# Other matrix products during attention as halves of 64 rows beside a score or a maximum

## The chip, the cores and the metric

The kernel runs on one core of a Trainium2 chip. TensorE multiplies matrices, VectorE and ScalarE read its results from PSUM, GpSimd works on SBUF alone, and SyncE (SP) issues transfers. The metric is the device time of one execution in microseconds (us), before: 1993.56, the median of three runs from 1993.28 to 1995.21.

## The reference, cut to what matters

The input has 2048 rows of 512. A condition vector gives six modulation rows; then comes one attention block of 32 heads of 16 and one mixer block with token shifts and an MLP.

```python
def _A_ref(x, wqkv, wo):
    qkv = (x @ wqkv).reshape(B, S, 3, H, Dh)...
    scores = jnp.einsum("bhqd,bhkd->bhqk", q, k) * (Dh ** -0.5)
    o = jnp.einsum("bhqk,bhkd->bhqd", _softmax(scores), v)
    return o... @ wo
def _B_ref(x, w1, w2, w3, w4):
    h = _gelu(_layernorm(x) @ w1)
    ...                                  # four column groups, shifted by +1, -1, +2, -2 rows
    x1 = x + hs @ w2
    return x1 + _gelu(_layernorm(x1) @ w3) @ w4
mod = (_silu(c) @ w_mod).reshape(c.shape[0], 6, 1, -1)
h = _layernorm(x) * (1 + ca) + sa
x = x + ga * _A_ref(h, A_wqkv, A_wo)
h = _layernorm(x) * (1 + cb) + sb
x = x + gb * _B_ref(h, B_w1, B_w2, B_w3, B_w4)
```

## The kernel before, in words

Every operand is kept as a high and a low part, and a full product is three matmuls per 128 rows of the sum (high by high, high by low, low by high; lines 361, 363 and 365), so a sum over 512 rows is 12 matmuls into one PSUM bank.

Attention runs over 64 units: four chunks of 512 queries, and 16 pairs of heads in each. The two heads of a pair lie on the two halves of the 128 rows: rows 0 to 63 hold one head's queries and keys, with their low parts and the shift, and rows 64 to 127 the other's. A unit has 16 steps over 128 keys. At each step TensorE makes, for both heads, the scores (tile `sc`, L1042), ScalarE writes their exponential into a probability tile (`pt`, L1038), GpSimd forms the low part of both heads at once (L1093; line 146 on ScalarE when GpSimd is behind), and TensorE adds up the weighted sum (`pv`, L1119 with the high part, L1116 with the low), four matmuls at a time on 32 columns each. The softmax's shift needs the maxima first: 24 steps ahead, TensorE makes other scores for maxima (`mb`, L1026), which VectorE reduces (`mx`, L1022). A score of one head and a maximum of the other head stand beside each other, as two products of 64 rows on the two halves of the array (`row_pair`).

All other matrix work of the program is fitted in between, as generators: the projections for later units (`q`, `k`, `v`), and for a chunk that is through attention the output projection (`wo`), the token mixer (`w1`, `w2`), the MLP (`w3`, `w4`) and transposes. They use all 128 rows of the array. Seven PSUM banks are shared by scores, maxima and these products; an eighth holds `pv`.

A planner in Python (`Sched`), run when the program is built, writes every instruction out in a fixed order per engine. It keeps a clock for each engine from a table of costs and has three modes for TensorE: `r` (row pairs), `c` (weighted sums) and `o` (others), with a planned cost for a change of mode (`SWITCH`, `ENTER`). `budget` pays credit per step from the due times `DUES`; in the loop, up to `GRP` row pairs are written as a burst, then weighted sums that are ready, or others as far as slack and credit go (`one` takes the next matmul of a generator).

```python
def row_pair(s, j):
    if 0 <= s < NS:
        parts.append((j, score_part(s, j)))
    if s + LEAD < NS:
        parts.append((1 - j, max_part(s + LEAD, 1 - j)))
```

The weights of these products come through a ring of three buffers (`wr`) on SP's queue, which also loads the keys, queries and V (`kst`, `qtl`, `vst`) in its order.

## Time and profile before

| | before |
|---|---|
| median of three runs | 1993.56 us |
| the profiled execution | 1993.19 us |
| its span (first to last instruction) | 1991.4 us |
| granted TensorE clock, mean | 0.991 |
| busy: TensorE, VectorE, ScalarE, GpSimd | 97%, 84%, 74%, 84% |
| TensorE matmuls in the profile | 14,480 |
| DMA, mean over the span | 147 GB/s |

A row of the groups reads: line, engine, operation, written tile `<-` read tiles, the shapes, the count; then busy time in us and the mean of one in ns; then the engine's idle time just before these instructions and what ended most of it. `64*128` before a matmul's shape are the rows and columns of the array that it uses. PEld is TensorE's weight load, shown as an engine of its own. The shown end of a matmul is modelled, so times between matmuls are read from start to start. A waits row reads: engine and line, what it waited for, us in total, how often, the longest.

### The profile page before, as it was taken

To read this page: it belongs to the slowest core of one execution; us is meant where nothing else is said; L and a number is where in the kernel's file an instruction comes from. 1 tells how busy PE (TensorE), PEld (TensorE's weight loads), DVE (VectorE), ACT (ScalarE), POOL (GpSimd) and SP (SyncE) were. 2 spreads that over 40 slices of the span, in tenths; PEclk is the share of its full clock that TensorE was granted. 3 is DMA by queue.
4 is the path that set the end of the run, shared out by engine and by line. 5 is a ranking of instruction groups with operands and counts; after the bars stand their busy time and mean duration, and the time that the engine had idled before them with its cause. 6 is when DMAs were issued, how large, how long until landed. Compare 5 with 4: busy or idle time off the path is not lost.

```text
span 1991.4 us, 42269 instructions
## 1 busy us (share of the span) xinstructions
PE 1933.8 (97%) x14480; PEld 1137.1 (57%) x14480; DVE 1669.9 (84%) x3010; ACT 1483.2 (74%) x3081; POOL 1671.0 (84%) x1601
## 2 busy tenths in 40 slices
PE   6989999999999999999999999999999999999899
PEld 4654565555445555555455555555555555555798
DVE  6969878899999888998999988888998888892643
ACT  5366888788878777787888877787888777786443
POOL 5368999999999998998898999888898988897532
PEclk8999999999999999999999999999999999999999
DMA  5675788786533433434433333344433334433432
GB/s 180 193 209 177 217 254 249 252 271 206 163 103 115 136 109 112 145 127 132 133 114 111 108 112 101 110 140 132 157 115 103 96 112 136 132 100 108 186 143 91
DMA packets 233082, 293.23 MB, mean 147 GB/s; under 512 B 125876, under 2 KB 178052, under 8 KB 216580
## 3 DMA queue, kind: packets, MB, share of 16 engines
q1 hardware_dynamic: 232868, 290.53, 45.8%
q8 instruction: 115, 1.88, 0.4%
q14 instruction: 99, 0.81, 0.1%
HBM read 225.81 MB, written 62.91 MB: 145 GB/s over the span
## 4 chain that ended last, share of the span: by engine, by line
PE 69%; DVE 9%; POOL 6%; ACT 6%; DMA 2%; issue 2%; SPq 1%; POOLq 0%; ACTq 0%; DVEq 0%
PE mb L1026 14%; PE sc L1042 11%; PE pv L1119 10%; PE w L361 7%; PE w L363 7%; PE w L365 7%; PE pv L1116 6%; DVE mx L1022 6%; POOL pt L1093 4%; ACT pt L1038 3%; PE ot L1151 1%; SPq L125 1%; DMA wr<-Ws 1%; PE q L365 1%; PE q L361 1%
## 5 line engine op out<-in xcount | busy, mean ns | idle before, releaser
L1022 DVE TENSOR_REDUCE mx<-mb 128x1 f32<-128x512 f32 x2048 | 1283.7, 682 | 117.2 <-PE mb L1026 88.6
L1093 POOL TENSOR_SCALAR pt<-pt 128x1024 f16<-128x1024 uint16 x980 | 1301.2, 1369 | 82.1 <-ACT pt L1038 78.6
L1038 ACT ACTIVATE pt<-sc 128x512 int32<-128x512 f32 x2048 | 1102.1, 602 | 272.5 <-PE mb L1026 181.2
L1026 PE MATMUL mb<-kst,qtl 64*128 64x512 f32 x2048 | 754.0, 455 | 18.3 <-DVE mx L1022 7.0
L1042 PE MATMUL sc<-qtl,kst 64*128 64x512 f32 x2048 | 728.3, 445 | 1.6 <-ACT pt L1038 0.7
L1026 PEld LDWEIGHTS mb<-kst,qtl 64*128 64x128 f32 x2048 | 347.1, 192 | 228.6 <-DVE mx L1022 108.4
L1042 PEld LDWEIGHTS sc<-qtl,kst 64*128 64x128 f32 x2048 | 334.9, 185 | 155.9 <-issue 52.5
L1119 PE MATMUL pv<-pt,vst 128*32 128x512 f16 x4096 | 348.8, 392 | 5.5 <-DMA vst<-Vs 4.9
L1116 PE MATMUL pv<-pt,vst 128*17 128x512 f16 (+1 forms) x2048 | 215.7, 397 | 4.6 <-POOL pt L1093 4.3
L1453 POOL TENSOR_TENSOR g<-xs,g 128x256 fp32r<-128x256 f32 (+2 forms) x144 | 103.4, 719 | 92.7 <-ACT g L1452 88.7
L1119 PEld LDWEIGHTS <-vst 128*32 128x32 bf16 x4096 | 112.3, 94 | 112.3 <-issue 48.1
L361 PE MATMUL w<-A,wr 128*128 128x256 f32 (+2 forms) x576 | 172.0, 299 | 0.6 <-ACT A L355 0.3
L363 PE MATMUL w<-A,wr 128*128 128x256 f32 (+2 forms) x576 | 170.0, 295 | 0.5 <-DVE A L351 0.3
L365 PE MATMUL w<-A,wr 128*128 128x256 f32 (+2 forms) x576 | 169.2, 294 | 0.0
L1116 PEld LDWEIGHTS <-vst 128*17 128x17 f16 (+1 forms) x2048 | 56.0, 90 | 130.5 <-issue 113.2
L361 PE MATMUL w<-wr,g 128*128 128x512 f32 x288 | 119.9, 416 | 0.8 <-ACT g L1452 0.6
L361 PEld LDWEIGHTS w<-A,wr 128*128 128x128 f32 x576 | 109.5, 190 | 18.0 <-issue 11.3
L365 PE MATMUL w<-wr,g 128*128 128x512 f32 x288 | 118.1, 410 | 0.2 <-POOL g L1453 0.2
L363 PEld LDWEIGHTS w<-A,wr 128*128 128x128 f32 x576 | 109.5, 190 | 14.4 <-issue 13.0
L363 PE MATMUL w<-wr,g 128*128 128x512 f32 x288 | 117.5, 408 | 0.0
L365 PEld LDWEIGHTS w<-A,wr 128*128 128x128 f32 x576 | 109.4, 190 | 12.9 <-issue 12.9
L1449 ACT ACTIVATE sq<-w 128x256 f32<-128x256 f32 (+2 forms) x144 | 55.8, 388 | 66.8 <-PE w L365 65.3
(150 smaller groups left out, 2095.6 us busy)
## 6 DMA issues: line engine op xcount, KB each, us to landing
wr<-Ws SPq DMA_DIRECT2D x80, 1024.0 KB
kst<-Ks SPq DMA_DIRECT2D x189, 256.0 KB
vst<-Vs SPq DMA_DIRECT2D x252, 192.0 KB
qtl<-Qs SPq DMA_DIRECT2D x192, 64.0 KB
Vs<-vt SPq DMA_DIRECT2D x32, 384.0 KB
Ws<-wq SPq DMA_DIRECT2D x40, 256.0 KB
Ws<-wst SPq DMA_DIRECT2D x40, 256.0 KB
wst<-in_B_w_dram SPq DMA_DIRECT2D x36, 256.0 KB
```

The lines of the kernel that those rows point to most:

```text
L361: te.matmul(o, lh, rh, start=first, stop=False)
L363: te.matmul(o, lh, rl, start=False, stop=False)
L365: te.matmul(o, ll, rh, start=False, stop=last)
L1022: end = sch.crit("D", 605, e + PX, lambda: dve.reduce_max(mxs[u][:, j, g, c:c + 1], b, axis=AX.X))
L1026: return ready, lambda: te.matmul(b, lhs, kst[u % 3][r, c * CH:(c + 1) * CH], start=True, stop=True), after
L1038: ea = sch.crit("A", 480, e + PX, lambda: act.activation(pt[s][:, j], b, AF.Exp))
L1042: return ready, lambda: te.matmul(b, kst[u % 3][r, kt * P:(kt + 1) * P], qst[u][r], start=True, stop=True), after
L1093: e_low[s] = XP["G"] + sch.crit("G", 1345, ready, lambda: pool.tensor_scalar(o, i, 0.5, 1.0, op0=OP.mult, op1=OP.mult))
L1116: te.matmul(acc[r:r + n, :], v[:, (kt + i) % 4, c - n:c].bitcast(F16), pt[s + i].bitcast(F16)[:, j, 0::2], start=False, stop=kt == NKT - 2 ...
L1119: te.matmul(acc[r:r + 32, :], v[:, kt % 4, r:r + 32], pt[s].bitcast(F16)[:, j, 1::2], start=kt == 0, stop=False, skip_group_check=True)
L1449: sch.chain(("A", cA(n), lambda: act.activation(sq, b, AF.Square, scale=2.0)), ("D", cD(n), cube), ("A", cA(n), lambda: act.activation(sq, ...
L1453: ("G", cG(n), lambda: pool.tensor_tensor(lo, xs, hi, op=OP.subtract)), (None, 0, end), bank=b)
```

## The change

During attention a sum of another product is no longer written as full matmuls. It becomes a `Group`: each of its matmuls is split in two of 64 rows, one on each half of the array, both adding into the same bank. The loop writes a half (`Group.half`, line 126) together with one score or maximum on the other 64 rows (`slot`). A product of 512 columns is one half per slot, of 256 columns two, of 128 columns four. All halves of one side can come first; when a sum goes over to the other side, a `drain` of TensorE is put ahead. What can't be paired is written whole (`Group.rest`, line 148), as is everything outside attention (line 448). The two row halves now have counters of their own (`yl`), up to `STAG` steps apart, so a score no longer needs a maximum beside it. One such sum is open at a time (`OPENS`). Planner constants go with it, among them `LACT`, how far GpSimd must be behind ScalarE before ScalarE forms a low part. Weights of the ring are released when the sums that read them are through (`settled`).

The built order has, in attention, 4832 halves, 443 drains and 666 matmuls that stay full. TensorE's order in the two places named below; names end in buffer numbers, and drains are not listed.

A product of `w3` with 256 columns, before: two row pairs, then the full product's matmuls.

```order
L1026 MATMUL mb_11624<-kst2_801,qtl2_799 128x512
L1042 MATMUL sc_11623<-qtl0_151,kst0_153 128x512
L1042 MATMUL sc_11631<-qtl0_151,kst0_153 128x512
L1026 MATMUL mb_11632<-kst2_801,qtl2_799 128x512
L363 MATMUL w3_11585<-A_10064,wr_10653 128x256
L365 MATMUL w3_11585<-A_10064,wr_10653 128x256
```

And now, behind the last matmul of a weighted sum: two halves, a score on the other rows, two halves, a maximum on the other rows.

```order
L1224 MATMUL pv_20303<-pt5_618,vst1_610 32x512
L126 MATMUL w3_20344<-A_18372,wr_20124 128x256 x2
L1139 MATMUL sc_20367<-qtl2_765,kst2_767 128x512
L126 MATMUL w3_20344<-A_18372,wr_20124 128x256 x2
L1122 MATMUL mb_20373<-kst0_153,qtl0_151 128x512
```

The matmuls of the product moved from a stretch of their own into the row stretch, two for one, and each score or maximum stands alone beside them.

A product of `w3` with 128 columns (it occurs in the first chunk alone), before:

```order
L1042 MATMUL sc_10175<-qtl0_151,kst0_153 128x512
L1026 MATMUL mb_10177<-kst2_801,qtl2_799 128x512
L361 MATMUL w3_10185<-A_9801,wr_9938 128x128
L363 MATMUL w3_10185<-A_9801,wr_9938 128x128
L365 MATMUL w3_10185<-A_9801,wr_9938 128x128
```

And now:

```order
L1122 MATMUL mb_11034<-kst2_767,qtl2_765 128x512
L126 MATMUL w3_10998<-A_10801,wr_10390 128x128 x4
L1139 MATMUL sc_11048<-qtl0_151,kst0_153 128x512
L126 MATMUL w3_10998<-A_10801,wr_10390 128x128 x4
L1139 MATMUL sc_11068<-qtl0_151,kst0_153 128x512
```

Here four halves stand beside one score.

The diff, cut to its core; the generators of the products now hand their list of matmuls to `summed`, and what followed a sum is passed along as a function.

```diff
-BTOP, BLOW = 1200.0, 300.0
+BTOP, BLOW = 1200.0, 100.0
...
-LACT = 800.0
+LACT = 4000.0
...
-EARLY, STAY, BACK, GRACE = 300.0, 300.0, 150.0, 0.0
-OWE, CTOP, OMIN, OMINC, OFIRST = 1500.0, 7000.0, 0.0, 800.0, 1500.0
-CHIGH, CMIN, CMOST, PTLOW, PLAG = 6500.0, 4, 6, 2, 1
...
+EARLY, BACK = 0.0, 400.0
...
+OWE, CTOP, CMIN, PTLOW = 0.0, 7000.0, 4, 1
+CTAKE, CIDLE = 0.0, 2
...
+STAG, OPENS = 4, 1
+DRAIN, FRESH = 150.0, 30.0
...
+class Group:
+    def __init__(self, sch, b, ops, m, t, fin):
+        self.sch, self.b, self.t, self.fin = sch, b, t, fin
+        self.parts = [ops[i:i + m] for i in range(0, len(ops), m)]
+        self.did, self.lane, self.done = [0, 0], None, False
+    def can(self, h):
+        return self.did[h] < len(self.parts)
+    def swaps(self, h):
+        return self.lane is not None and self.lane != h
+    def left(self, h):
+        return self.did[h] < len(self.parts)
+    def half(self, h):
+        r = slice(64 * h, 64 * h + 64)
+        ops = self.parts[self.did[h]]
+        first = not sum(self.did)
+        self.did[h] += 1
+        swap = self.swaps(h)
+        self.lane = h
+        last = sum(self.did) == 2 * len(self.parts)
+        for i, (lhs, rhs) in enumerate(ops):
+            if swap and not i:
+                self.sch.te.drain()
+            self.sch.te.matmul(self.b, lhs[r], rhs[r], start=first and not i, stop=last and i == len(ops) - 1, skip_group_check=True)
+        self.sch.credit -= self.t / 2
+        self.sch.spent += self.t / 2
...
+    def rest(self):
+        sch, n = self.sch, len(self.parts)
+        lag = self.did.index(min(self.did))
+        if self.did[0] != self.did[1]:
+            sch.to("r")
+            while self.did[0] != self.did[1]:
+                self.half(lag)
+                sch.T["P"] += self.t
+        while self.did[0] < n:
+            i = self.did[0]
+            for k, (lhs, rhs) in enumerate(self.parts[i]):
+                sch.te.matmul(self.b, lhs, rhs, start=not i and not k, stop=i == n - 1 and k == len(self.parts[i]) - 1, skip_group_check=True)
+            self.did = [i + 1, i + 1]
+            sch.spend(self.t)
...
+    def summed(nm, n, get, fin, ahead=None):
+        yield sch.room
+        b = dbank(nm)[:, :n]
+        ops, m = get(), CH // n
+        if not sch.carrying:
+            for i, (lhs, rhs) in enumerate(ops):
+                te.matmul(b, lhs, rhs, start=not i, stop=i == len(ops) - 1)
+                yield nsq(n)
+            fin(b)
+            return
+        g = Group(sch, b, ops, m, m * nsq(n), fin)
+        yield g
...
+    def slot(hs, g):
 
         parts = []
-        if 0 <= s < NS:
-            parts.append((j, score_part(s, j)))
-        if s + LEAD < NS:
-            parts.append((1 - j, max_part(s + LEAD, 1 - j)))
-        parts = [x for _, x in sorted(parts, key=lambda x: x[0])]
-
-        def mms():
-            for _, mm, _ in parts:
+        for h in sorted(hs):
+            k, i = divmod(yl[h], 2)
+            yl[h] += 1
+            parts.append((max_part if i else score_part)(k + LEAD * i, h))
+        if g:
+            def mms(mm=parts[0][1]):
+                g.half(1 - hs[0])
                 mm()
-        e = sch.put("P", CROW, max(x[0] for x in parts), mms)
-        return [partial(x[2], e) for x in parts]
+            if g.swaps(1 - hs[0]):
+                sch.T["P"] += FRESH if sch.fresh else DRAIN
+            e = sch.put("P", max(CROW, g.t), parts[0][0], mms)
+            g.close()
+        else:
+            e = sch.put("P", CROW, max(x[0] for x in parts), lambda: [x[1]() for x in parts])
+        sch.fresh = False
+        for x in parts:
+            x[2](e)
+        if second:
+            second.pop(0)()

...
+    def part(h):
+        while yl[h] < end:
+            k, i = divmod(yl[h], 2)
+            if i and k + LEAD >= NS or not i and k < 0:
+                yl[h] += 1
+                continue
+            break
+        if yl[h] >= end or k > seen + STAG:
+            return False
+        if i:
+            return (k + LEAD) // NKT in qst
+        if ("shift", k // NKT) not in done:
+            return None
+        return k in pt or bool(pts)
...
+        if sch.credit > CTAKE:
+            while not all(any(g.left(h) for g in sch.groups) for h in range(2)) and sch.one():
+                if sch.T["P"] > now:
+                    break
+            if sch.T["P"] > now:
+                fillers()
+                continue
+        ok = [part(h) for h in range(2)]
+        low = int(yl[1] < yl[0])
+        if sch.mode != "r":
+            lane = low
+        hs, g = [], None
+        if sch.credit > CTAKE:
+            for h in (lane, 1 - lane):
+                g = ok[h] and next((g for g in sch.groups if g.can(1 - h)), None)
+                if g:
+                    hs = [h]
+                    break
+        if not g:
+            hs = [h for h in (low, 1 - low) if ok[h]]
...
+        cap = nc_ == len(pvs) or nc_ >= CMOST or nc_ and not pvs[nc_][1] and pvs[nc_][0] % NKT == 0
+        want = sch.mode == "r" and not g and sch.groups and sch.credit > CTAKE
+        if nc_ and (cap or nc_ >= CMIN and len(pts) <= PTLOW or not hs or nc_ >= CIDLE and (want or slack > 0 and room >= nc_ * CCOL + 2 * SWITCH + ENTER - BACK)):
+            do_cols(nc_)
+        elif hs and slack <= 100.0:
+            sch.to("r")
+            sch.T["P"] = max(sch.T["P"], one)
+            if g:
+                lane = hs[0]
+            late = sorted(e_exp)
+            slot(hs, g)
+            for q in late:
+                p_low(q)
+        elif hs:
+            sch.T["P"] = now + 50.0
...
```

More of the change, by code (lines that the diff above doesn't have):

```diff
@@ L107, in __init__ @@
         self.end = 0.0
-        self.mode = None
+        self.mode, self.te, self.carrying = None, None, False
+        self.groups, self.fresh, self.opens = [], False, set()
         self.banks(8)
@@ L201, in add, with spend, one @@
         self.gens.insert(len(self.gens) if at is None else at, [gen, None])
-    def one(self):
+    def spend(self, v):
+        self.credit -= v
+        self.spent += v
+        if self.mode:
+            self.to("o")
+        self.T["P"] += v
+    def one(self, force=False):
         self.marks()
+        if self.groups and (force or not self.carrying) and self.groups[0].rest():
+            return True
         for g in list(self.gens):
@@ L301, in step @@
             self.misc(e, max(t, self.T[e]) + 500)
-        while self.T["P"] < t and self.one():
+        while self.T["P"] < t and self.one(True):
             pass
@@ L1008, in bank @@
         return x, ap_.tile([P, CH], F32, name=nm, tag=f"s{x}", bufs=1)
+    left = {}
     def max_part(m, j):
@@ L1378, in norm_T, with wo_out @@
             yield from transposed(lambda k, j: xn[key, ts[j]][:, k * P:(k + 1) * P], range(KT), len(ts), A)
[L1380 to L1392 removed]
+        def wo_out(b, i, t):
             x1 = x1t[t]
@@ L1647, in do_cols @@
     def do_cols(n):
+        while second:
+            second.pop(0)()
         sch.to("c")
@@ L1680 @@
-        now, row, slack = sch.T["P"], False, LATE
-        if can:
-            need = (s >= 0) + (s + LEAD < NS)
-            sch.flush(need)
-            free = sorted(sm.t)
-            one = free[need - 1 + 2 * (s < 0)]
+            before(seen)
+            sch.credit = max(min(sch.credit + budget(seen), CTOP), -OWE)
+        sch.flush(2)
+        now = sch.T["P"]
+        if sch.credit > CTAKE:
[5 more added lines that the diff above has]
+                continue
@@ L1686 @@
+        slack = room = LATE
+        if hs:
+            one = free[len(hs) - 1]
             if one >= LATE:
-                one = free[need - 1]
-            enter = (sch.mode != "r") * (SWITCH + ENTER)
+                one = free[0]
+                hs = hs[:1]
+            slack = one - enter - now
+            room = max(one, sch.T["D"] - CROW - PX - EARLY) - now
         else:
@@ L1694 @@
         nc_ = cols()
-        if can:
-            if sch.mode == "r" and burst < GRP:
-                slack = one - now
-                row = slack <= STAY
-            else:
-                st = one
-                for k in range(2, GRP + 1):
-                    if need * k <= len(free) and free[need * k - 1] < LATE:
-                        st = max(st, free[need * k - 1] - (k - 1) * CROW)
-                dry = sch.T["D"] if s + LEAD < NS else sch.T["A"]
-                slack = max(st, dry - CROW - PX - EARLY) - enter - now
-                row = slack <= BACK and (sch.mode == "r" or sch.credit < CHIGH and not (nc_ >= CMIN and len(pts) <= PTLOW))
```

252 lines of the change are left out of this document (120 added, 132 removed).

## The prediction, made before the result was known

> **What bounds the kernel now.** I read the page first: the share of each engine, the chain that ended last, and the costliest groups.
>
> ```profile
> span 1991.4 us, 42269 instructions
> PE 1933.8 (97%) x14480; PEld 1137.1 (57%) x14480; DVE 1669.9 (84%) x3010; ACT 1483.2 (74%) x3081; POOL 1671.0 (84%) x1601
> PE 69%; DVE 9%; POOL 6%; ACT 6%; DMA 2%; issue 2%; SPq 1%; POOLq 0%; ACTq 0%; DVEq 0%
> L1022 DVE TENSOR_REDUCE mx<-mb 128x1 f32<-128x512 f32 x2048 | 1283.7, 682 | 117.2 <-PE mb L1026 88.6
> L1093 POOL TENSOR_SCALAR pt<-pt 128x1024 f16<-128x1024 uint16 x980 | 1301.2, 1369 | 82.1 <-ACT pt L1038 78.6
> ```
>
> TensorE holds 69% of the chain, and 97% "busy" is no measure of what is left, because the ends of matmuls are modelled and overlap. VectorE and GpSimd are at 84% each over the span. So two things can set attention's length: how densely TensorE's order is packed, and how steadily the two other engines are fed. The list by tile dates attention: the first row of maxima at 63.3 us, the last matmul of the weighted sum at 1828.4 us.
>
> ```profile
> L1026 PE MATMUL mb<-kst,qtl x2048: 383/498/792, 63.3 to 1791.2; 64*128 64x512 f32 x187
> L1116 PE MATMUL pv<-pt,vst x2048: 385/397/423, 107.4 to 1828.4; 128*17 128x512 f16 x95, 128*25 128x512 f16 x92
> ```
>
> That is 1765 us. A timeline of TensorE shows what a step costs; the first column is the start, and the differences of starts are what counts.
>
> ```profile
> 1299.66 0.40 PE L1119 MATMUL pv<-pt,vst 128*32 128x512 f16 x4
> 1299.99 0.49 PE L1042 MATMUL sc<-qtl,kst 64*128 64x512 f32 x1
> ...
> 1300.34 0.62 PE L1042 MATMUL sc<-qtl,kst 64*128 64x512 f32 x2
> 1300.56 0.39 PE L1026 MATMUL mb<-kst,qtl 64*128 64x512 f32 x1
> 1300.88 0.50 PE L363 MATMUL w<-wr,g 128*128 128x512 f32 x1
> 1301.22 0.40 PE L365 MATMUL w<-wr,g 128*128 128x512 f32 x1
> 1301.45 0.60 PE L1151 MATMUL ot<-ident,ac 128*128 128x128 f32 x4
> ...
> 1303.20 0.28 PE L365 MATMUL w<-A,wr 128*128 128x256 f32 x1
> 1303.33 0.28 PE L361 MATMUL w<-A,wr 128*128 128x256 f32 x1
> 1303.53 0.50 PE L1026 MATMUL mb<-kst,qtl 64*128 64x512 f32 x1
> ```
>
> A pair of row products, or one full product of 512 columns, follows the last in 0.22 to 0.23 us (1300.34 to 1300.56, 1301.22 to 1301.45): I call 0.23 a slot. From rows to full products it takes 0.32 (1300.56 to 1300.88), so the switch costs 0.09, and the second product then starts 0.34 behind the first, another 0.11: 0.20 together. From the weighted sum to rows it is 0.33 and then 0.35: 0.10 + 0.12, so 0.21 on the mean. A switch to the weighted sum I price at 0.10, like the first part of the others.
>
> The program's order, counted from the first maximum to the last weighted sum, has 827 stretches of rows, 447 of full products, 516 of weighted sums; 2062 row slots; 1922 full slots (984,064 columns); 1536 groups of four weighted-sum products. So: 3984 x 0.23 = 916; 1536 x 0.23 = 353; switches 827 x 0.21 + 447 x 0.20 + 516 x 0.10 = 315; and 14 for narrow products (below). That is 1598 us; the other 167 us of the 1765 are waits.
>
> ```profile
> ACT pt L1038 <- PE mb L1026: 181.2, 250, 3.0
> ...
> PEld mb L1026 <- DVE mx L1022: 108.4, 299, 1.9
> ...
> DVE mx L1022 <- PE mb L1026: 88.6, 169, 2.3
> POOL pt L1093 <- ACT pt L1038: 78.6, 124, 3.7
> ACT pt L1038 <- PE sc L1042: 70.1, 102, 2.9
> ...
> PE pv L1119 <- DMA vst<-Vs: 4.9, 3, 2.7
> ```
>
> The waits go both ways: TensorE waits for VectorE to free a bank (108.4), while ScalarE, VectorE and GpSimd wait for products and for each other. That is the picture of a bursty order: three row pairs arrive in 0.7 us, and then a run of full products or weighted sums brings nothing.
>
> **The change, part by part.** *Switches.* In the changed order there are 557 stretches of rows, 103 of full products, 498 of weighted sums. Saved: 270 x 0.21 + 344 x 0.20 + 18 x 0.10 = 57 + 69 + 2 = 128 us.
>
> *Slots.* 4832 half products stand in the row stretches (3260 half slots of 512 columns), 137,216 columns (268 slots) stay full. If both halves of the array were always filled, nothing would change. They are not: walked through in order, with each half of the rows taking its own products, the row stretches need 3848 slots where 3678 would do. With the 268, that is 4116 against 3984: +132 x 0.23 = +30 us. No row of before shows a half product beside a score. The nearest is the score beside the maximum at 1300.34, two 64-row products in one slot; I take that. Instructions: 2416 more matmuls, each with its own weight load. The loads of the two row halves start together:
>
> ```profile
> 1005.08 0.19 PEld L1026 LDWEIGHTS mb<-kst,qtl 64*128 64x128 f32 x1 [0.24 <-DVE mx L1022]
> 1005.08 0.18 PEld L1042 LDWEIGHTS sc<-qtl,kst 64*128 64x128 f32 x1
> 1005.19 0.19 PEld L1026 LDWEIGHTS mb<-kst,qtl 64*128 64x128 f32 x1
> ```
>
> and the next on the same half 0.11 later. A slot whose half product comes as two of 256 columns needs two loads on that side, 0.22 in 0.23: it just fits, so 0 extra.
>
> *Narrow products.* A product of 256 columns follows in 0.12 to 0.13 (1303.20 to 1303.33), 0.005 over half a slot. One of 128 columns takes 0.11, twice its share:
>
> ```profile
> 703.08 0.28 PE L365 MATMUL w<-A,wr 128*128 128x128 f32 x1
> 703.19 0.28 PE L361 MATMUL w<-A,wr 128*128 128x128 f32 x1
> ```
>
> Before, 168 of these cost 168 x 0.053 = 9 us over their slots. Now 336 halves go four to a slot, which lasts 0.44 instead of 0.23: 84 x 0.21 = 18, so +9. The 1320 slots of two 256-wide halves last 0.24 instead of 0.23 (+12, where the full ones cost some 6): +6. Together +15 us.
>
> *Drains.* 443 stand in attention, and none before, so the price has to be bounded. 230 follow a weighted sum, where the switch empties the array anyway; 213 stand among row products. Low: nothing behind a switch, and 0.09 among rows, the first part of a switch: 19 us. High: a matmul shown for 0.40 whose successor starts after 0.23 has 0.17 to run; then a first matmul is shown 0.11 longer (0.50 against 0.39), and the second follows 0.11 late: 0.39 among rows, 0.17 behind a switch: 83 + 39 = 122 us. I take a whole switch (0.20) among rows, since that also empties and refills the array, and 0.05 behind one: 43 + 12 = 54 us. Queued behind a drain stands all of TensorE's order: the score beside it, then its exponential on ScalarE, the low part on GpSimd, and the weighted sum. The Trainium skill (TensorEngine Tiling, Key Properties) says that changing the tiling mode drains TensorE. By that the 230 behind a switch would cost nothing and the sum would be 12 us less; the 0.09 of the row-to-full switch agrees with a drain there, but no row shows an explicit one.
>
> TensorE's own work thus changes by -128 + 30 + 15 + 54 = -29 us, to 1569. From the drains' bounds: -64 to +39.
>
> *Waits.* 344 of 447 runs in which no score comes are gone, so the 88.6 and 181.2 above should shrink. How far the others can follow is read from the windows (busy PE, PEld, DVE, ACT, POOL):
>
> ```profile
> 400.00:800.00 400.00, 392.25 (x3043) 212.77 (x3041) 363.33 (x647) 323.19 (x666) 372.23 (x349) 1.00 0.47 151
> 800.00:1200.00 400.00, 396.14 (x3121) 218.71 (x3121) 362.50 (x660) 324.62 (x674) 361.43 (x348) 1.00 0.39 122
> 1200.00:1600.00 400.00, 395.07 (x3103) 221.07 (x3101) 360.88 (x654) 318.00 (x658) 360.72 (x347) 1.00 0.38 119
> 450.00:500.00 50.00, 49.78 (x376) 25.25 (x368) 46.41 (x76) 40.13 (x80) 48.14 (x41) 1.00 0.63 205
> 500.00:550.00 50.00, 49.24 (x405) 23.71 (x402) 48.40 (x84) 43.77 (x88) 47.73 (x41) 1.00 0.58 181
> ```
>
> From 400 to 1600 us GpSimd is busy 1094 of 1200 (91%), VectorE 1087. The best stretch, 450 to 550, has GpSimd at 95.9 of 100. At that pace the 1200 would last 1094 / 0.959 = 1141: at most -59 there. The remaining 565 us of attention are less loaded on these engines; I give them only TensorE's share, 29 x 565 / 1765 = 9. So the limit set by the others is -68, and the waits can fall by 39 at most. Against it: the two exponentials of a probability tile stand further apart in the new order (2.1 scores on the mean, 1.5 before), so each of the 8 tiles is held longer. I take 25 of the 39.
>
> *The rest.* Behind attention stand 12,288 more columns, 24 slots: +5.5 us, uncovered, since that stage is full products alone. The raised threshold for handing the low part to ScalarE moves the count from 980 to 976 on GpSimd: 4 x 1.4 = 5 us there, inside its 9% slack. The loads of the next weights are issued when a sum is settled; SP's queue waits in order, with the V, Q and K loads behind:
>
> ```profile
> SPq L125 <- PE w L365: 194.2, 42, 19.0
> ```
>
> TensorE now waits 4.9 us for V in all, since those loads are asked for a unit ahead; that lead is the cover, and I take 0. Were it gone, the wait would at most repeat what SP's queue now loses on one such product, 194.2 / 42 = 4.6 us each time.
>
> **Sum.** -29 - 25 + 5.5 = -48.5. The profiled execution was 1993.19 us (span 1991.4 and 1.8 around it), 0.4 under the median of 1993.56, so 1945 us either way.
>
> **Rivals.** *A, as forecast:* 1915 to 1975, chance 0.47.
>
> *B, the drains are cheap and the others keep up:* drains 19 instead of 54 and waits down the full 39: another 49 less, near 1896, 1880 to 1915. For it: GpSimd does reach 96% where TensorE leaves it room. Against: all three long windows have GpSimd at 90 to 93% (360.72 to 372.23 of 400), and the 96% is of one short stretch. 0.15.
>
> *C, slower, by the drains:* each stops TensorE's order until the array is empty. At the high price they cost 122: TensorE +39, waits perhaps 10 less, +5.5, so about 2028, 1996 to 2040. It decides from 0.23 us per drain on the mean: (128 - 45 + 25 - 5.5) / 443. For it: nothing in the trace prices a stop of the sequencer; against: the switches, which empty the array too, show 0.20. 0.17.
>
> *D, slower, by the weight loads:* the second 256-wide half cannot load beside the first on the same rows, +0.11 in each of 1320 slots: +145, about 2090 (1945 + 145). Against: 256-wide full products follow in 0.13 on the same rows, load hidden. 0.04. The Trainium skill (TensorE: Matmul & The Clock Gate, Part 3) has a load overlap a running matmul only when the row group differs, which would give this case; the trace's 0.13 does not show it.
>
> *E, the change does not feed the others better:* what TensorE saves comes back as waits, because probability tiles finish in clusters and GpSimd starves and then queues. Waits +10 to +25 instead of -25: 1975 to 1996, mean about 1985. For it: POOL already waits 78.6 for the exponentials. 0.17, of which 0.09 is faster, 0.08 the same.
>
> **Numbers.** The measurement cannot tell less than about 0.2% (4 us) from no change. Faster 0.47 + 0.15 + 0.09 = 0.71, same 0.08, slower 0.17 + 0.04 = 0.21. The range runs from 1895, which leaves out the better half of B, to 2020, which takes in most of C's lower half; D and the rest of C are left out.
>
> **What would show it.** Right: about 100 full stretches; scores and halves starting within one 0.23 slot; at a side change a gap near 0.4 between starts; ScalarE's and VectorE's waits for TensorE well under 181 and 89; GpSimd above 93% from 400 to 1600. Wrong: slots of 0.3 or more with two 256-wide halves (D); gaps over 0.6 at side changes (C); GpSimd's wait for the exponentials grown past 100 us (E).

## The result: 2062 us against 1994, and the profile after

The changed kernel takes 2062.49 us (median of four, 2059.99 to 2064.31); the kernel before, on the same chip, 1994.38. The ratio is 1.034, with an interval from 1.0322 to 1.0358. The forecast was 1945, in a range from 1895 to 2020. It was wrong in sign.

The page of the changed kernel, the same rows as before:

```profile
span 2062.5 us, 47512 instructions
PE 1932.1 (94%) x16896; PEld 1245.4 (60%) x16896; DVE 1665.2 (81%) x3010; ACT 1494.8 (72%) x3089; POOL 1660.7 (81%) x1597
PE 75%; DVE 10%; DMA 4%; issue 4%; ACT 3%; SPq 3%; POOL 2%; POOLq 0%; ACTq 0%; DVEq 0%
L1117 DVE TENSOR_REDUCE mx<-mb 128x1 f32<-128x512 f32 x2048 | 1292.6, 683 | 194.9 <-PE mb L1122 127.6
L1198 POOL TENSOR_SCALAR pt<-pt 128x1024 f16<-128x1024 uint16 x976 | 1293.0, 1368 | 162.1 <-ACT pt L1135 157.4
```

TensorE's part of the chain of waits has grown from 69% to 75%, and the other engines are less busy than before. So TensorE's order got slower, and the others wait for it more. The waits say the same:

```profile
ACT pt L1135 <- PE sc L1139: 241.2, 335, 6.8
...
POOL pt L1198 <- ACT pt L1135: 157.4, 161, 11.2
DVE mx L1117 <- PE mb L1122: 127.6, 221, 5.6
...
PE sc L1139 <- DMA qtl<-nm: 26.9, 7, 7.7
PEld mb L1122 <- DVE mx L1117: 26.1, 70, 1.0
```

TensorE's own wait for a bank, the last of these rows, has shrunk from 108.4 to 26.1. VectorE's wait for a maximum rose from 88.6 to 127.6, GpSimd's for the exponentials from 78.6 to 157.4, and a row is new: a score waits for the shift (`nm`, written into `qtl` by a transfer), seven times, 26.9 us. The list by tile dates attention:

```profile
L1122 PE MATMUL mb<-kst,qtl x2048: 383/393/794, 61.9 to 1855.7; 64*128 64x512 f32 x187
L1221 PE MATMUL pv<-pt,vst x2048: 385/397/632, 108.2 to 1892.1; 128*17 128x512 f16 x96, 128*25 128x512 f16 x91
```

It lasts 1892.1 - 61.9 = 1830 us, where it was 1765: +65. What lies behind it went from 1991.4 - 1828.4 = 163.0 to 2062.5 - 1892.1 = 170.4, +7.4 (forecast +5.5). So the loss is in attention.

**Where attention's 65 us come from.** I laid the built order beside the start of every matmul in the trace and added up, for both kernels: the products one after the other as the order has them, two sides at once; the switches at the prediction's 0.21, 0.20 and 0.10; the drains at the median that their places show (below); the rest is waits. (The stretches are counted without the few products of the condition vector, `mr` and `vb`; with them the order has 827, 447, 516 and 557, 103, 498, exactly the prediction's counts.)

| us in attention | before | after | difference | forecast |
|---|---|---|---|---|
| products, in order | 1286 | 1328 | +42 | +45 |
| switches (824, 441, 516 stretches; then 548, 90, 498) | 313 | 183 | -130 | -128 |
| drains (213 among rows, 230 behind a switch) | 0 | 123 | +123 | +54 |
| waits, the rest | 166 | 196 | +30 | -25 |
| sum | 1765 | 1830 | +65 | -54 |

The first two rows come as forecast, but they are the order's counts at the prediction's prices and no separate measurement. The traces bear the prices out: a slot takes 0.233 us with a 512-wide half and 0.234 with two of 256 (medians of 1286 and 863), 0.447 with four of 128 (forecast 0.44), and a bare switch from the weighted sum to rows 0.324, where it was 0.325. What they do not settle is whether the two sides of the array wait for each other: if each side ran on its own, the products would take some 1290 us instead of 1328, and the waits some 38 more. The other two rows missed by 69 and 55.

**What a drain costs.** A piece of the timeline of the changed kernel holds both kinds:

```profile
1300.22 0.41 PE L1221 MATMUL pv<-pt,vst 128*17 128x512 f16 x4
1300.72 0.38 PE L126 MATMUL w<-A,wr 64*128 64x256 f32 x1
1300.73 0.49 PE L1139 MATMUL sc<-qtl,kst 64*128 64x512 f32 x1
1300.94 0.39 PE L126 MATMUL w<-A,wr 64*128 64x256 f32 x2
1301.06 0.39 PE L1122 MATMUL mb<-kst,qtl 64*128 64x512 f32 x1
1301.17 0.40 PE L126 MATMUL w<-A,wr 64*128 64x256 f32 x2
1301.30 0.39 PE L1139 MATMUL sc<-qtl,kst 64*128 64x512 f32 x1
...
1302.00 0.39 PE L1122 MATMUL mb<-kst,qtl 64*128 64x512 f32 x1
1302.01 0.91 PE L126 MATMUL w<-A,wr 64*128 64x256 f32 x3
1302.55 0.50 PE L1122 MATMUL mb<-kst,qtl 64*128 64x512 f32 x1
...
1302.89 0.39 PE L1139 MATMUL sc<-qtl,kst 64*128 64x512 f32 x1
```

From 1301.06 to 1301.30 a maximum, a score and four halves run at 0.23 per slot: the halves themselves are as cheap as forecast. From 1302.00 to 1302.55 the sum changes side, with a drain: 0.55 where 0.23 would do, and the next slot takes 0.34. Over all 213 such drains the median is 0.297 beyond the slot at the drain and 0.105 at the next: 0.40 each. Behind the weighted sum the rows start after 0.50 (1300.22 to 1300.72), where the same switch took 0.33 before (1299.66 to 1299.99): over 230 of them the median beyond the last product is 0.262, against 0.098 bare, so 0.164 each. 213 x 0.40 + 230 x 0.164 = 85 + 38 = 123. That is 0.278 per drain on the mean, over the 0.23 from which rival C decides. The starts also show how a drain differs from a switch. Behind a bare switch the next product starts 0.07 us before the shown end of the last one (1299.99 against 1299.66 + 0.40 above, and so at the median of every kind of bare switch, in both kernels); behind each of the 443 drains it starts after that end, by 0.13 at the median among rows and 0.09 behind a weighted sum.

**The stalls.** Four times TensorE stood still for 6 to 8 us in the middle of attention, three times for a shift and once for keys (`kst`); before, no gap after the first 200 us was over 2. One of the three, first SP's queue and then TensorE:

```profile
1141.62 1.73 SPq L186 DMA_DIRECT2D qtl<-Qs  x3
1143.40 0.61 SPq L186 DMA_DIRECT2D qtl<-zero  x1
1144.05 1.74 SPq L186 DMA_DIRECT2D kst<-Ks  x3
1145.84 0.58 SPq L186 DMA_DIRECT2D vst<-Vs  x1
1146.52 5.02 SPq L186 DMA_DIRECT2D qtl<-nm  x8
```

```profile
1143.02 0.50 PE L126 MATMUL w<-wr,g 64*128 64x512 f32 x1
1151.08 0.76 PE L1139 MATMUL sc<-qtl,kst 64*128 64x512 f32 x1 [7.56 <-DMA qtl<-nm]
```

The eight transfers of the shift stand on SP's queue behind the loads of the next unit; the first score of the unit cannot start before they have landed. The row halves now run up to four steps apart, so the last maximum of a unit comes later, measured against that score: in the built order 17 scores stood between the two before, 14 at the median and 11 at the least now. From the shift's final reduction on VectorE to the first score the median was 12.75 us before (the shortest 8.3), and is 10.2 (6.2) now. And behind each stall the clock falls. The windows around this one:

```profile
1143.00:1151.00 8.00, 0.52 (x2) 0.18 (x1) 0.85 (x2) 0.00 (x0) 3.29 (x3) 0.74 0.52 149
...
1151.00:1160.00 9.00, 8.83 (x43) 5.22 (x45) 4.46 (x9) 4.68 (x8) 3.33 (x5) 0.50 0.18 44
1160.00:1162.00 2.00, 1.90 (x18) 0.84 (x16) 1.87 (x3) 1.74 (x4) 2.00 (x3) 0.87 0.00 0
```

The granted clock (third number from the end) stays at 0.50 for 9 us. So such a stall costs its 7.5 us and, by an estimate from these rows, another 4 or so (9 us at half the clock). The Trainium skill (TensorE: Matmul & The Clock Gate, Part 1) has the clock fall after one idle window of about 3.4 us, and come back after a busy one; the fall agrees, the 9 us are longer than one window.

The slower clock is part of the row of waits, and not only behind the stalls. By the clock records of the traces it stands at 0.50 during 106 us of attention now, and during 17 us before. The first 24 of the 106, from 65 to 89 us, cost little: VectorE is busy there almost throughout, and the first score comes at 90.1 us, before at 97.5. The other 82 can have cost 41 us at most, against 8.5 before. So the 30 us need not all be time spent waiting for another engine.

### The profile page after: what moved, and what is told of

Same layout as the page of the kernel before. It is cut to its first block, busy times and chain, and to the rows that moved or that the text cites. A ratio compares the mean times of both kernels' runs of the same rounds, so it can differ in the third digit from the quotient of the medians.

```text
span 2062.5 us, 47512 instructions
## 1 busy us (share of the span) xinstructions
PE 1932.1 (94%) x16896; PEld 1245.4 (60%) x16896; DVE 1665.2 (81%) x3010; ACT 1494.8 (72%) x3089; POOL 1660.7 (81%) x1597
## 4 chain that ended last, share of the span: by engine, by line
PE 75%; DVE 10%; DMA 4%; issue 4%; ACT 3%; SPq 3%; POOL 2%; POOLq 0%; ACTq 0%; DVEq 0%
PE w L126 21%; PE pv L1224 11%; PE sc L1139 8%; PE mb L1122 8%; PE pv L1221 7%; PE w L448 6%; DVE mx L1117 6%; PE q L126 3%; SPq L186 3%; PE wo L126 3%; PE k L126 2%; PE ot L1256 2%; PE v L126 1%; ACT pt L1135 1%; DMA qtl<-nm 1%
## 5 line engine op out<-in xcount | busy, mean ns | idle before, releaser
L1117 DVE TENSOR_REDUCE mx<-mb 128x1 f32<-128x512 f32 x2048 | 1292.6, 683 | 194.9 <-PE mb L1122 127.6
L1198 POOL TENSOR_SCALAR pt<-pt 128x1024 f16<-128x1024 uint16 x976 | 1293.0, 1368 | 162.1 <-ACT pt L1135 157.4
L1139 PE MATMUL sc<-qtl,kst 64*128 64x512 f32 x2048 | 811.7, 431 | 32.4 <-DMA qtl<-nm 26.9
L1122 PE MATMUL mb<-kst,qtl 64*128 64x512 f32 x2048 | 822.4, 438 | 13.2 <-DMA kst<-Ks 5.6
L1122 PEld LDWEIGHTS mb<-kst,qtl 64*128 64x128 f32 x2048 | 377.9, 196 | 70.8 <-DVE mx L1117 26.1
L126 PE MATMUL w<-A,wr 64*128 64x256 f32 (+1 forms) x2472 | 365.4, 289 | 20.3 <-PE mb L1122 0.2
L126 PEld LDWEIGHTS w<-A,wr 64*128 64x128 f32 x2472 | 311.4, 187 | 113.1 <-issue 105.0
L126 PE MATMUL w<-wr,g 64*128 64x512 f32 x1052 | 302.3, 416 | 14.4 <-DVE xs L1554 0.2
L126 PEld LDWEIGHTS w<-wr,g 64*128 64x128 f32 x1052 | 184.4, 188 | 113.9 <-issue 89.5
L126 PE MATMUL q<-hT,wp 64*128 64x512 f32 x310 | 89.6, 418 | 4.4
L126 PE MATMUL v<-wp,hT 64*128 64x256 f32 x504 | 86.4, 317 | 3.5
L126 PEld LDWEIGHTS v<-wp,hT 64*128 64x128 f32 x504 | 73.0, 209 | 22.4 <-issue 19.2
L126 PE MATMUL wo<-wr,A 64*128 64x512 f32 x288 | 82.4, 412 | 3.7
```

Of the source, the lines that this page charges most:

```text
L126: self.sch.te.matmul(self.b, lhs[r], rhs[r], start=first and not i, stop=last and i == len(ops) - 1, skip_group_check=True)
L1117: end = sch.crit("D", 605, e + PX, lambda: dve.reduce_max(mxs[u][:, j, g, c:c + 1], b, axis=AX.X))
L1122: return ready, lambda: te.matmul(b, lhs, kst[u % 3][r, c * CH:(c + 1) * CH], start=True, stop=True), after
L1139: return ready, lambda: te.matmul(b, kst[u % 3][r, kt * P:(kt + 1) * P], qst[u][r], start=True, stop=True), after
L1198: e_low[s] = XP["G"] + sch.crit("G", 1345, ready, lambda: pool.tensor_scalar(o, i, 0.5, 1.0, op0=OP.mult, op1=OP.mult))
```

## The experiments

All are measured against the kernel before on the same chip; the intervals are 95%. The letters in the expectations name the readings that each one states, not the prediction's rivals, unless it says so. Waits of a run are worked out as in the table above.

### What the drains cost, without the rest of the change

```diff
+            if sch.behind:
+                te.drain()
+            sch.behind = False
             for _, mm, _ in parts:
                 mm()
...
+        sch.behind = True
         del pvs[:n]
```

> The kernel before with 512 drains added, each ahead of the first row pair behind a weighted sum (458 straight behind it, 54 with full products between); nothing else differs. Theory D (the drains cost what the changed kernel's trace shows, 0.16 us over the bare switch, and nothing absorbs it): 512 x 0.16 = 82 us more, 2060 to 2080. Rival W (the order of TensorE has room, since 166 us of attention are waits, and the others set the time): less than 30 us more, under 2025.

Measured: 2060.38, ratio 1.0336 [1.0318, 1.0355]. Attention 1832. A drained switch shows 0.282 beyond the last product, a bare one 0.098, so 512 x 0.184 = 94 us were added to TensorE's order, and 67 us came through. The waits of this run are 139, 27 less than before, so that is where the rest went. With nothing else changed, drains alone make the kernel as slow as the whole change did, and behind a switch they are not free.

The second test keeps the change and takes its drains away. In the change a drain stands wherever a sum goes over to the other side, since both sides add into one bank; here the halves of rows 64 to 127 go into a bank of their own that nobody reads, once with and once without drains:

```diff
-NSM = 7
+NSM = 6
...
-            self.sch.te.matmul(self.b, lhs[r], rhs[r], ...
+            self.sch.te.matmul(self.bs[h], lhs[r], rhs[r], ...
...
-            if swap and not i:
+            if swap and not i and False:          # the second run alone
                 self.sch.te.drain()
```

> The changed kernel, but the halves of rows 64 to 127 of a split sum add into a bank of their own that nobody reads (so these sums lack half of their products), and six banks instead of seven are shared; the drains stay (202 among rows, 244 behind a switch). It is the partner of the next one. Both theories: one bank fewer costs something, 2065 to 2110.

> The same as the run with two banks and drains, in the same order, with every drain in attention left out; these sums lack half of their products too. Theory D: 202 x 0.40 + 244 x 0.16 = 120 us, so 90 to 125 us less than with the drains. Rival W: less than 40 us less.

Measured: 2109.07, 1.0574 [1.055, 1.0598], with drains; 2042.07, 1.0239 [1.022, 1.0257], without. The 446 drains are worth 67.0 us net, 0.15 each: less than the 90 to 125 of theory D, more than the 40 of rival W. At the same 185 places of the same order, the slot in which a sum goes over to the other side takes 0.561 us with the drain and 0.235 without (medians), so the price belongs to the drain and not to the change of sides. And one shared bank fewer, with the order planned anew for six, costs 2109 - 2062 = 47.

### The lead of the maxima

```diff
-LEAD = 24
+LEAD = 26
```

> The changed kernel with the maxima 26 steps ahead of the scores instead of 24; 448 drains instead of 443. Theory S (part of the loss are scores that wait for the shift rows, which SP issues behind the loads of the unit two later; four stalls of 6 to 8 us and the halved clock behind each): no stall over 5 us at a unit's first score, 30 to 45 us less than the changed kernel's 2062, so 2017 to 2032. Theory D alone: within 10 us of 2062.

Measured: 2031.25, 1.0197 [1.0172, 1.0223]. No first score of a unit waits for its shift over 5 us any more, the median from reduction to score is 14.3 us, and the row for the shift is gone from the waits. Attention is 1795, its waits 162 instead of 196: about what they were before the change (166). So the rise of the waits by 30 goes with these stalls and the clock behind them; 68 us of attention still have the clock at 0.50.

### Fewer drains, or dearer ones for the planner

With the longer lead, the planner was told the measured prices, and the loop was made to keep a side until a weighted sum comes anyway (the first two lines of the diff alone are the second run):

```diff
-DRAIN, FRESH = 150.0, 30.0
+DRAIN, FRESH = 400.0, 165.0
...
-            lane = low
+            g = next((g for g in sch.groups if g.lane is not None and g.can(g.lane)), None)
+            lane = low if g is None else 1 - g.lane
...
+        if g and sch.mode == "r" and g.swaps(1 - hs[0]):
+            nc_ = cols()
+            if nc_:
+                do_cols(nc_)
...
```

> The changed kernel with the maxima 26 steps ahead, the planner's prices of a drain raised to 400 and 165 ns, and a sum that keeps its side when rows are entered again and changes it only behind a weighted sum: 4 drains among rows and 222 behind a switch instead of 197 and 251 of the run with 26 steps. Against it, the two exponentials of a tile stand 3.6 scores apart instead of 2.1, there are 79 more row stretches, and 24,000 more columns lie behind attention. Theory D: 81 us of drains go, half of it or more is kept: 1985 to 2005. Theory E (tiles held longer take back what TensorE saves): 2015 to 2045.

Measured: 2080.71, 1.0441 [1.0419, 1.0463], slower than with the longer lead alone, although only 226 drains are left, 222 of them of the cheap kind. There are 15 gaps over 2 us, 45 us in sum beyond a slot each, where the changed kernel has 6 with 35: staying on one side lets the two row halves drift apart, to 3.6 scores between the two exponentials of a tile, and six of the gaps end with a load of keys or V, one with a shift. The run lies outside both expectations, and its cause is not shown: the gaps are only 35 us more than with the longer lead alone, while the waits of attention rise from 162 to some 260.

> The changed kernel with the maxima 26 steps ahead, and the planner told what a drain was measured to cost: 400 among rows and 165 behind a switch, in place of 150 and 30. Its order has 208 drains among rows and 241 behind a switch, 549 stretches of rows, 488 of weighted sums, where the one with 26 steps alone has 570 and 505. If the planner's clock ran ahead of the chip by its cheap drains and so issued rows before their banks were free, the waits fall and it comes 15 us or more below 2031. If the drains are simply paid (theory: gross price, number unchanged), it stays between 2020 and 2035.

Measured: 2028.54, 1.0177 [1.0138, 1.0216], no different from 2031. The prices in the planner's table were too low, but that costs nothing: the drains are simply paid.

### Do tiles, or the distance of the row halves, starve the others?

The longer lead and the unread bank together, without drains; then with the row halves at most one step apart; and, with drains, one probability tile fewer:

```diff
-STAG, OPENS = 4, 1
+STAG, OPENS = 1, 1          # the second of the three
...
-NPT = 8
+NPT = 7                     # the third
```

> The run with two banks and no drain (half of the split sums' products go to a bank that nobody reads), with the maxima 26 steps ahead. Theory S: the two stalls of 10 us at a unit's first score go, 20 to 35 us less than 2042, so 2007 to 2022. If drains had been what made the lead too short: within 8 us of 2042.

> The same without drains and with 26 steps, but the two row halves may be one step apart instead of four, so the two exponentials of a tile stand 1.4 scores apart instead of 2.1 (1.5 in the kernel before). Without drains, changing sides costs nothing here. Theory E (tiles held longer starve GpSimd and the weighted sums): 15 to 40 us less than the run with four steps. Rival (the halves alone fill TensorE, the distance is free): within 8 us.

> The changed kernel with the maxima 26 steps ahead and seven probability tiles instead of eight; 468 drains instead of 448. Theory E: tiles are what is short, 25 us or more over the run with eight (2031). Rival: within 10 us of it, the 20 more drains making 3.

Measured: 2028.02 (1.0173 [1.0152, 1.0195]), 2033.89 (1.0202 [1.0183, 1.0221]) and 2025.16 (1.0156 [1.0141, 1.0172]). Attention is 1795 in the first two alike, so the distance of the halves costs nothing by itself. Seven tiles are not slower than eight. That speaks against the mechanism of rival E, tiles held longer that finish in clusters. Without drains the longer lead gains 14 us only (2042 to 2028), short of the 20 to 35 expected; with them it gains 31.

### The shared banks

In the kernel before:

```diff
-NSM = 7
+NSM = 6
```

> The kernel before with one edit: the pool that row maxima, scores and sums share has six banks instead of seven. Its program keeps the same work; its order has 1070 stretches of rows (827 before), 534 of full products (447), 595 of weighted sums (516). Theory S (the shared banks set how far the order can be packed, so one bank less is dear in any order): the switches alone are 243 x 0.21 + 87 x 0.20 + 79 x 0.10 = 76 us, and the waits of TensorE for a bank (108 us for the maxima) grow by 20 or more beside them: 2090 or later. Rival W (the waits belong to GpSimd and VectorE; TensorE's extra 76 us are partly taken out of the waits, as two thirds only of the drains' gross 94 us came through in the kernel before with drains): 2040 to 2050. In the changed kernel the loss of one bank cost 47 us (2109 against 2062).

Measured: 2104.84, 1.0551 [1.053, 1.0572], so +112. The built order has 76 us more of switches by the prediction's prices, and its waits are 202 where they were 166. Banks set how far an order can be packed, and here one bank is dearer than the 512 drains above. The change opens no bank more, and holds one for a sum, from its first product to its last, during 77% of attention where it was 72%.

### The threshold of the low parts

First the old threshold in the changed kernel with the longer lead (the other constant, `BLOW`, is put back too; it leaves TensorE's order in attention as it is), then the new threshold in the kernel before:

```diff
-LACT = 4000.0
+LACT = 800.0
```

> The changed kernel with the maxima 26 steps ahead, and two numbers of the planner as they stood before: a low part goes to ScalarE when GpSimd is late by 800 instead of 4000, and 300 instead of 100 at BLOW. In its order GpSimd has 728 low parts instead of 976, the other 248 are ScalarE's, and there are 599 stretches of rows, 536 of weighted sums, 416 drains in attention (570, 505 with 26 steps alone). Rival G (the raised threshold left GpSimd with more than it can do in time, so that probability tiles come late): GpSimd loses 248 x 1.37 = 340 us of its work, its wait list and TensorE's waits shrink, and it comes to 2000 or less. Theory D+S (drains, the shorter lead of the maxima and the shared banks): GpSimd has slack already, the extra switches cost 29 x 0.21 + 31 x 0.10 = 9, fewer drains give some 7 back: 2025 to 2040.

> The kernel before with LACT at 4000, as the change has it, and nothing else. The built order has 813 stretches of rows (827), 432 of full products (447) and 501 of weighted sums (516); GpSimd forms 999 low parts instead of 980. By the prices of the prediction the switches give 14 x 0.21 + 15 x 0.20 + 15 x 0.10 = 7 us, and 19 x 1.37 = 26 us move to GpSimd, out of ScalarE's 38 fewer halves. Theory N (the threshold matters only where the new loop would send 248 tiles to ScalarE; in the kernel before it hardly binds): 1984 to 1996. Rival H (a low part on ScalarE delays the exponentials behind it, in any order): a gain of more than 10 us, 1980 or less.

Measured: 2126.81 (1.0664 [1.0631, 1.0698]) and 1996.76 (1.0009 [0.9999, 1.002]). The first is 95 us slower than with the new threshold, against both expectations. Its rows for ScalarE and a wait:

```profile
L1135 ACT ACTIVATE pt<-sc 128x512 int32<-128x512 f32 x2048 | 1132.6, 613 | 127.5 <-PE sc L1139 94.5 <-PE mb L1122 14.2 <-PE w L126 11.8
L206 ACT ACTIVATE pt<-pt 128x512 f16<-128x512 uint16 x592 | 464.6, 797 | 1.3
```

```profile
POOL pt L1198 <- ACT pt L1135: 453.7, 407, 4.2
```

ScalarE makes 592 half low parts of 0.797 us instead of 96, and each stands ahead of exponentials on its queue. From the start of a score's product to the end of its exponential it is now 1.87 us on the mean, 1.47 with the new threshold, and for that time the score holds its bank. GpSimd idles 453.7 us for exponentials. So GpSimd's load is not the limit, since it is busy 1354.6 us instead of 1661.1 and the kernel is slower. ScalarE is busy 1767.5 us, 83% of the span, where it is 1492.5 (74%) with the new threshold; whether its load or the longer hold of the bank makes the 95 us, these runs do not separate. In the kernel before the threshold hardly binds and does nothing.

### Who makes the waits

The work of VectorE, ScalarE and GpSimd on each tile is halved; orders, matmuls, transfers and drains stay.

```diff
-dve.reduce_max(mxs[u][:, j, g, c:c + 1], b, axis=AX.X)
+dve.reduce_max(mxs[u][:, j, g, c:c + 1], b[:, :CH // 2], axis=AX.X)
...
-act.activation(pt[s][:, j], b, AF.Exp)
+act.activation(pt[s][:, j, :CH // 2], b[:, :CH // 2], AF.Exp, scale=0.02)
...
-                o, i, 0.5, 1.0, op0=OP.mult, op1=OP.mult))
+                o.rearrange("p (j n) -> p j n", j=2)[:, :, :CH // 2], i.rearrange("p (j n) -> p j n", j=2)[:, :, :CH // 2], 0.5, 1.0, ...
```

> The kernel before, its order unchanged, with the other engines' work on each tile halved: the maximum is taken over 256 of a product's 512 columns, the exponential and the low part over 256 of 512 columns too (the exponent is scaled and shifted so that it stays finite; the other columns keep a constant). Every matmul, DMA and bank stays. So half of the maxima, exponentials and low parts is left out. VectorE loses some 2048 x 0.33 = 680 us, ScalarE 2048 x 0.25 = 500, GpSimd 980 x 0.65 = 640. Theory K (the waits of TensorE in attention are made by the other three engines): most of its 166 us of waits go, attention falls from 1765 to 1610 to 1660, the time to 1840 to 1890. Rival P (they are TensorE's own: gaps at starts, loads of K and Q, the order): less than 60 us go, 1935 or later.

> The same halving (half of the maxima, exponentials and low parts left out) in the changed kernel with the maxima 26 steps ahead; its order, its 468 drains and its banks stay. TensorE's own work by the stretches: 1291 streaming, 187 switches, 115 for drains beyond them: 1593. Theory K: the 203 us of waits fall to 60 or less, attention from 1796 to 1600 to 1650, the time to 1840 to 1890, level with the kernel before with the same halving, since the change saves TensorE 130 in switches and pays 7 + 115. Rival P: less than 70 us go, 1960 or later.

> The same halving in the kernel without drains and with the maxima 26 steps ahead (halves of rows 64 to 127 into a bank that nobody reads, six shared banks; half of the split sums is left out as well). TensorE's own work: 1283 streaming, 192 switches: 1475; 319 of waits at full work. Theory K: the waits fall below 100, attention from 1795 to 1530 to 1590, and it comes to 1760 to 1830, 60 or more below the other two: with idle consumers the saved switches do come through, and it is the consumers that took the saving back. Rival P: 1900 or later.

Measured: 1912.83 (0.9591 [0.9575, 0.9607]), 1960.13 (0.9825 [0.981, 0.9839]) and 1890.01 (0.9471 [0.9454, 0.9488]). The first and the last lie between the two readings, the second on the edge of rival P. (The kernel with the longer lead has 448 drains; the 468 in its expectation are those of the run with seven tiles.) In the kernel before 82 of 166 us of waits go (attention 1683), with the longer lead 69 of 162 (attention 1726), without drains 140 of 272 (attention 1655). Now the other engines wait for TensorE several times as long as before; in the first of the three and then in the second:

```profile
ACT pt L1040 <- PE mb L1028: 426.8, 459, 4.0
POOL pt L1095 <- ACT pt L1040: 393.6, 460, 3.8
DVE mx L1024 <- PE mb L1028: 361.9, 471, 3.8
```

```profile
POOL pt L1200 <- ACT pt L1137: 449.4, 391, 8.7
ACT pt L1137 <- PE sc L1141: 395.4, 457, 8.2
DVE mx L1119 <- PE mb L1124: 355.1, 448, 7.0
```

The difference of the first two comes out of the same account: 1960.13 - 1912.83 = 47, where products in order give +41, switches -126, drains +120, waits +9 and the stage behind attention +9.5 (163.4 to 172.9): 53, and the two profiled executions differ by 52. So about half of the waits go when the other engines' work is halved; what they make of the other half is not shown. The kernel with drains loses here too, with VectorE busy for 62% of the span, ScalarE and GpSimd for 57%. How much of that is TensorE's own work hangs on the account: with each side of the array on its own, the products are +7, as the expectation has them, and the waits +43.

| run | us | ratio |
|---|---|---|
| the change | 2062 | 1.034 |
| before, with 512 drains | 2060 | 1.034 |
| two banks, with drains / without | 2109 / 2042 | 1.057 / 1.024 |
| lead 26 | 2031 | 1.020 |
| lead 26, sides changed behind sums / dearer drains | 2081 / 2029 | 1.044 / 1.018 |
| lead 26, seven tiles / old threshold | 2025 / 2127 | 1.016 / 1.066 |
| lead 26, two banks, no drains / and one step apart | 2028 / 2034 | 1.017 / 1.020 |
| before, six banks / new threshold | 2105 / 1997 | 1.055 / 1.001 |
| half work: before / lead 26 / two banks, no drains | 1913 / 1960 / 1890 | 0.959 / 0.983 / 0.947 |

Among the kernels that compute all of it, none beats the one before.

## Why the prediction was wrong, by its own steps

**The switches** were priced right: a bare switch costs what it did, and the counts are those of the order. **The slots and narrow products** too: +42 against +45 in order, though only some +7 if the two sides need not keep the order (the last section). With two 256-wide halves a slot still takes 0.23, so rival D is out.

**The drains** are the first step that failed: "I take a whole switch (0.20) among rows, since that also empties and refills the array, and 0.05 behind one". They cost 0.40 and 0.164, together 123 us of TensorE's time instead of 54 (some 67 us net, by the two-bank pair). That is the high bound of the prediction: 0.39 and 0.17, 122 us. That bound was worked out from the rows (a matmul shown for 0.40 whose successor starts after 0.23 has 0.17 to run, and then a new start is paid), and it describes what a drain does: it waits for the shown end of the last product, while a switch lets the next product in before. The nearest row, the switch, was the wrong one to take: behind it the next product starts 0.07 before that end, behind a drain 0.09 to 0.13 after it. The sentence cited from the Trainium skill (TensorEngine Tiling, Key Properties), by which the 230 behind a switch would cost nothing, is not borne out for explicit drains: 0.164 each.

**The waits** are the second: "the waits can fall by 39 at most ... I take 25 of the 39". They rose by 30. What the step had against a fall, the distance of the two exponentials of a tile, costs nothing (the one-step run and the seven tiles). What raised them, with the slower clock behind it, is not in the prediction at all: the shift of a unit comes late by SP's queue when its last maximum comes late, and 24 steps of lead no longer cover it; 26 do, and 31 us come back. The prediction had costed SP's queue for V and for the weights, not for the shift. But with 26 steps the waits are only level with before, so the fall of 25 did not come either, and the runs with halved work show why it was no safe term: only half of them go even when the other engines' work is halved.

**That the terms add up** was a silent step, and by whole runs the dearest. Time taken from TensorE's order comes through in part: of 94 us of drains in the kernel before 67 showed, of some 120 in the two-bank pair 67. The rest came out of the waits. So the 130 us of saved switches need not have been worth 130 either. With two banks, leaving out the drains and lengthening the lead gave 2109 - 2028 = 81 together. By that, the changed kernel without drains and with the longer lead would be near 2062 - 81 = 1981 (an estimate; no run has seven banks and no drains), where the forecast without its drains says 1945 - 54 = 1891. So drains and stalls explain why the change is slower than the kernel before (81 against a loss of 68), but 90 of the 117 us between forecast and result lie elsewhere: of the 103 us that the other terms promised, some 13 came. Why the saved switches bring so little stays open.

**The threshold** was costed at nothing, with GpSimd's slack as its cover. In the kernel before that holds (1.0009). What the step missed is that in the new loop the old threshold would have sent 248 tiles to ScalarE, 95 us; the change needed that edit.

**Behind attention** +7.4 against +5.5: right.

**The rivals.** C had the place, the sign and the point of decision: 0.23 per drain, measured 0.278. Its TensorE account of +39 is +35 in the table. It ends at 2028 and not at 2062 because it lets the waits fall by 10 where they rose by 30. E forecast a rise of the waits, by 10 to 25, and its sign came (GpSimd's wait for the exponentials is past 100, at 157.4), but two runs speak against its mechanism. Of the signs named beforehand, with the windows of the changed kernel from 400 to 1600 us in sum,

```profile
sum 1200.00, PE 1132.57 PEld 695.55 DVE 1042.65 ACT 931.96 POOL 1047.82; mean PE 377.52 PEld 231.85 DVE 347.55 ACT 310.65 POOL 349.27
```

the 103 full stretches, which the order fixes, and two products per 0.23 slot came; the gap of 0.4 at a side change was 0.55, nearer to C's 0.6; the waits of ScalarE and VectorE, and GpSimd's share (1048 of 1200, 87%, instead of over 93%), went the wrong way.

Not tried: the kernel before with a lead of 26, so what that would give there stays open. Nor were the other planner constants of the diff (`EARLY`, `BACK`, `OWE`, `PTLOW` and their like) put back, so their part in the loss is not known.

## What to carry to other kernels

An operation that the trace has never shown, and that holds an engine until its work ahead is done, should be priced from the shown end of that work plus a fresh start, not from the nearest operation that lets work overlap; with hundreds of them the price can decide the sign. When a change moves when a result is ready relative to its first use, look up every transfer between the two on an in-order queue, since a lead that was just long enough turns into stalls of several us, and each of these here also cost the clock. Time added to or taken from the busiest engine comes through in part where buffers couple it to others: here 67 us of 94 and of some 120. So a forecast that adds up terms of one engine should give its sum a discount, and a range for that.

## What the runs showed of the hardware

- An explicit drain of TensorE among 64-row products costs 0.297 us at its place and 0.105 at the next product; behind a switch from four column tiles to two row tiles, 0.164 to 0.184 over the bare switch. Without it, a sum goes over to the other row half in an ordinary slot (0.235).
- Behind a bare switch the next product starts 0.07 us before the shown end of the last; behind a drain, 0.09 to 0.13 after it.
- Products on the two row halves do not keep the program's order in their starts. At 1300.72 the order is half, half, score; the score starts at 1300.73, and the second half, ahead of it in the program, at 1300.94. The Trainium skill (TensorE: Matmul & The Clock Gate) has matmuls start and end strictly in program order; by these records that does not hold between row halves.
- After a stall of 7.6 us the granted clock stayed at 0.50 for 9 us.
